# Windowed attention and a SiLU MLP on one core: the first MLP product of the last four token groups made of 7 products of quarters for 8

## The chip, the cores and the metric

One core of a Trainium2 chip runs the whole program. The metric is the device time of one execution in microseconds (us), lower is better, as the median of several runs. TensorE (PE) multiplies, VectorE (DVE) and ScalarE (ACT) work on whole tiles, GpSimd (POOL) takes some elementwise work, and SyncE (SP) issues the transfers.

## What is computed

```python
# attention, 8 batches x 8 heads, 576 positions, head size 64, float32
scores = scale * q @ k^T + bias           # only where 0 <= row - col < 128
attn   = softmax(scores)
x      = (attn @ v) as [4608 tokens, 512]
# MLP
h   = x @ w_in                            # [4608, 512] @ [512, 2048]
g   = h * sigmoid(h)
out = g @ w_out                           # [4608, 2048] @ [2048, 512]
```

## The kernel before

The tokens are cut into 36 tiles of 128 and these into nine groups of 512 tokens (`g` = 0 to 8). For every group the MLP goes through 16 blocks `f` of 128 hidden units. `gemm1` makes the block's hidden values `h` (128 hidden units by 512 tokens) in PSUM, `act1` to `act4` make of them the activated values, and `gemm2` multiplies these with the block's part of `w_out` into four PSUM tiles (`ops`, tags w, x, y, z) that gather over all 16 blocks; `store` scales and writes them. A float32 operand is split into two parts, high and low, and each product is made of three: high by high, high by low, low by high. From group 3 on all of these parts are float16 (`w16`, and `gh`, `gl` for the activated values). So `gemm1` takes, for a block, 4 slices of 128 model dimensions times 3 products, 12 matmuls of 512 columns each; group 2 moves the same columns in pieces of 256 (two matmuls with the same weights, each with a weight load of its own). `gemm2` takes 12 matmuls of 512 columns too. A group has 384 such matmuls.

Attention of group `g + 1` runs inside the MLP of group `g`, one pair (a tile of 128 tokens and four of its heads) for every two blocks. The order of all engines' work is written out by hand: the position `pos` counts half products (64 positions a group), `at(p)` is the position at which pair `p` is begun, and `put` and `later` file each further step under a position. `begin()` issues what is filed for a position, ahead of that position's matmuls. Each engine works through its instructions in the order in which they were issued.

A pair's steps are `scores` (TensorE, into two PSUM tiles of tag a), `row_max` (VectorE), `exps` (ScalarE), `p_hi` and `p_lo` (a float16 split), two transposes by DMA (`p_transpose`), `attend` (TensorE, into one more tile of tag a; this tag has two buffers), `normalize` (VectorE, two stages: the row's divisor, then the division, which frees the tile of tag a), and `x_hi` and `x_lo`, the float16 split of the result. `x_dma` then transposes a finished tile of x, one transfer for each tile from group 1 on, so that it stands ready (tile `xt`) when its group begins. `v_hi` (GpSimd) and `v_lo` (VectorE) split the attention's values, ahead of `attend`. PSUM tag h has two buffers; one block's `h` fills one.

The chain between the products of a block is ScalarE's tanh (L487), VectorE's multiply (L492), ScalarE's float16 copy (L502) and VectorE's remainder (L508). `gemm2` of block `f` is issued behind `gemm1` of block `f + 1`.

Of the kernel before, what the change touches and what calls it, by code (L numbers as in the profile page):

```python
# [16 lines left out]
P = 128  # L17
# [12 lines left out]
TG = 512  # L30
# [33 lines left out]
def at(p):  # L64

    if p < 2 * GT:
        return STEP * (p - 2 * GT) - 18
    if p < 4 * GT:
        return CLOSE[p - 2 * GT]
    return STEP * (p - 2 * GT) - LEAD  # L70


@with_exitstack
def tile_window_attention_then_silu_mlp(ctx, tc, qk, v, w_in, w_out, base8, out):
# [92 lines left out]
    def vscale_finish(b, stage):  # L167

        r, name = vred[b], "".join(str(c) for c in b) if isinstance(b, tuple) else b
        if stage == 0:  # L170
            r["col"] = col = pool.tile([P, 3], F32, tag="vcol", name=f"vcol{name}")
            nc.vector.tensor_reduce(col[:, 0:1], r["m"], axis=AX.X, op=ALU.max)
        elif stage == 1:
            col = r["col"]
            ps = ps_of(next_tag("misc"), f"vt{name}")
            nc.tensor.transpose(ps[:1, :P], col[:, 0:1], ident)
            c = col[:1, 1:2]
            nc.vector.tensor_reduce(c, ps[:1, :P], axis=AX.X, op=ALU.max)
# [9 lines left out]
            nc.vector.tensor_single_scalar(inv.bitcast(I32), c.bitcast(I32), -(14 << 23), op=ALU.add)  # L188
            nc.vector.tensor_scalar(c.bitcast(I32), c.bitcast(I32), -1, 268 << 23, op0=ALU.mult, op1=ALU.add)
# [446 lines left out]
    def put(point, fn, *a):  # L636
        plan.setdefault(max(point, at(0)), []).append((fn, a))

    for p in range(NPAIR):
        i, q = divmod(p, 2)  # L640
        n = at(p)
        if p == 2 * GT - 1:
            a = n + 2 * STEP - 1
        elif p == 2 * GT:
            a = n + 10
        elif p == 2 * GT + 1:
            a = n + 12
        else:
# [32 lines left out]
        put(z + 2, x_lo, p)  # L681
        if q == 0:
# [31 lines left out]
    def later(n, fn, *a):  # L714
        put(pos[0] + n, fn, *a)
# [137 lines left out]
```

## Time and profile before

| | before |
|---|---|
| median of 3 runs | 987.19 us (985.68 to 987.44) |
| the profiled execution, its own time | 983.54 us |
| its span, from the first to the last instruction | 981.8 us |
| mean granted TensorE clock | 0.985 of full speed |

The profile comes from one execution, which was 3.65 us shorter than the median of the three timed runs; 1.7 us of its own time lie around the span. Rows give start and duration in us, or a mean in ns. Matmuls are pipelined and their ends are modelled, so the time that a run of matmuls takes is read from the start of one row to the start of the next.

### The profile page before, as it was taken

Reading aid. Unit: us, or ns where it says so; the run is one execution under the profiler, and the core shown is the slowest. Engines: PE = TensorE matmul, PEld = TensorE weight load, DVE = VectorE, ACT = ScalarE, POOL = GpSimd, SP = SyncE. Lnnn points to the kernel's source line nnn. Section 1 sums busy time; section 2 is a strip of 40 time slices with the busy share of each in tenths; the row PEclk is TensorE's granted clock in tenths of the full one; section 3 lists DMA queues with packets and bytes.
Section 4 is the critical chain, followed back from the end, with each engine's and each line's share of the span. In section 5 each row is a group of like instructions: output and inputs, shape, how many; then the busy total and the mean of one; then the engine's idle time right before and its main releaser. Section 6 shows DMA issues by size and latency. Waiting matters only on the chain.

```text
span 981.8 us, 17277 instructions
## 1 busy us (share of the span) xinstructions
PE 943.0 (96%) x6572; PEld 581.3 (59%) x6572; DVE 625.8 (64%) x1599; ACT 481.9 (49%) x984; POOL 100.2 (10%) x97
## 2 busy tenths in 40 slices
PE   7878889899998999999999999999999999999998
PEld 6756667677776887654555554555555545554443
DVE  4888999755666887776666665554655565553222
ACT  4656666677444554555454444444544454433222
POOL 3112123122111222100000000000000000000000
PEclk8998999999999999999999999999999999999999
DMA  7258886723324542432364545332433343331001
GB/s 233 80 167 222 225 209 186 183 65 86 71 70 129 119 119 76 119 86 65 87 151 118 119 97 129 87 86 65 130 86 87 86 129 87 65 54 54 1 1 43
DMA packets 201074, 104.94 MB, mean 107 GB/s; under 512 B 168224, under 2 KB 176416, under 8 KB 200992
## 3 DMA queue, kind: packets, MB, share of 16 engines
q1 hardware_dynamic: 200992, 103.84, 41.5%
q8 instruction: 52, 0.85, 0.4%
q14 instruction: 30, 0.25, 0.1%
HBM read 54.00 MB, written 9.44 MB: 65 GB/s over the span
## 4 chain that ended last, share of the span: by engine, by line
PE 78%; DVE 12%; DMA 4%; ACT 3%; issue 2%; SPq 1%; POOL 0%; ACTq 0%; DVEq 0%; POOLq 0%
PE o L540 32%; PE h L474 30%; PE sp L278 6%; PE h L479 4%; PE av L368 4%; DVE wm L581 2%; DVE t L298 1%; DVE wm L576 1%; DMA wr<-w_in 1%; DVE gt L492 1%; DMA wr<-w_out 1%; DVE hr L322 1%; DVE wol L595 1%; DVE v L260 1%; DMA hl<-hr 1%
## 5 line engine op out<-in xcount | busy, mean ns | idle before, releaser
L474 PE MATMUL h<-xt,wi 128*128 128x512 f16 (+1 forms) x1536 | 317.8, 354 | 0.0
L487 ACT ACTIVATE gt<-h,gsc 128x512 f32<-128x512 f32 x112 | 77.0, 688 | 318.5 <-PE h L474 316.4
L540 PE MATMUL o<-wo,gh 128*128 128x512 f16 x768 | 228.4, 379 | 0.0
L474 PEld LDWEIGHTS <-wi 128*128 128x128 f16 x1536 | 143.6, 98 | 130.8 <-issue 2.2
L492 DVE SCALAR_TENSOR_TENSOR gt<-gt,h 128x512 f32<-128x512 f32 x144 | 98.6, 685 | 174.4 <-ACT gt L487 174.1
L540 PE MATMUL o<-wo,gl 128*128 128x512 f16 x384 | 145.6, 379 | 0.0
L540 PEld LDWEIGHTS <-gh 128*128 128x128 f16 x768 | 74.8, 98 | 88.6
L308 ACT ACTIVATE t<-t,mx 128x256 f32<-128x256 f32 (+1 forms) x288 | 121.3, 486 | 8.5 <-DVE mx L298 8.5
L508 DVE SCALAR_TENSOR_TENSOR gl<-gt,gh 128x512 f16<-128x512 f32 x96 | 66.4, 692 | 74.8 <-ACT gh L502 74.7
L298 DVE CUSTOM_DVE_ANT_0 t<-sp,tab 128x256 f32<-128x256 f32 (+1 forms) x288 | 102.2, 402 | 18.3 <-PE sp L278 18.0
L322 DVE SCALAR_TENSOR_TENSOR hr<-t,hr 128x512 f16<-128x512 f32 (+1 forms) x128 | 93.5, 748 | 21.4 <-ACT hr L317 21.4
L510 POOL TENSOR_TENSOR gl<-gt,gh 128x512 fp32r<-128x512 f32 x45 | 62.1, 1379 | 287.4 <-ACT gh L500 230.9
L278 PEld LDWEIGHTS sp<-k,q 64*128 64x128 f32 x1088 | 68.8, 190 | 31.9 <-issue 30.2
L278 PE MATMUL sp<-k,q 64*128 64x128 f32 x1088 | 83.2, 289 | 4.6 <-DVE xs L395 4.1
L502 ACT ACTIVATE gh<-gt 128x512 f16<-128x512 f32 x96 | 60.0, 625 | 47.5 <-DVE gt L492 47.2
L540 PE MATMUL o<-woh,gh 128*128 128x512 f32 x192 | 79.2, 413 | 0.7 <-DVE mx L298 0.4
L368 PE MATMUL av<-v,hl 128*128 128x65 f16 (+1 forms) x1632 | 63.9, 195 | 16.1 <-DVE mx L298 10.7
L368 PEld LDWEIGHTS <-hl 128*128 128x128 f16 x1632 | 59.5, 99 | 32.6 <-issue 20.6
L540 PE MATMUL o<-woh,gl 128*128 128x512 f32 x192 | 76.8, 400 | 1.6 <-POOL gl L510 1.6
L317 ACT ACTIVATE hr<-t 128x512 f16<-128x512 f32 (+1 forms) x128 | 75.8, 598 | 1.1 <-DMA hl<-hr 1.1
L540 PE MATMUL o<-wol,gh 128*128 128x512 f32 x192 | 76.3, 398 | 0.0
L249 POOL TENSOR_SCALAR v<-rv,vsc 128x512 f16<-128x512 f32 x32 | 27.6, 861 | 443.7 <-DMA rv<-v 262.0
(108 smaller groups left out, 977.1 us busy)
## 6 DMA issues: line engine op xcount, KB each, us to landing
q<-qk SPq DMA_DIRECT2D x36, 256.0 KB, 3.0
k<-qk SPq DMA_DIRECT2D x36, 256.0 KB, 3.1
vm<-v SPq DMA_DIRECT2D x36, 256.0 KB, 3.6
out<-ot SPq DMA_DIRECT2D x36, 256.0 KB, 2.3
wr<-w_in SPq DMA_DIRECT2D x16, 512.0 KB, 4.0
wr<-w_out SPq DMA_DIRECT2D x16, 512.0 KB, 3.9
rv<-v SPq DMA_DIRECT2D x32, 256.0 KB, 2.9
hl<-hr SPq DMA_TRANSPOSE x128, 2.8
```

The lines of the kernel that those rows point to most:

```text
L278: nc.tensor.matmul(sp[h][:, u, o], qs[i][rows, 2 * q + u], ks[i - 1 + o][rows, 2 * q + u], start=True, stop=True, skip_group_check=True,)
L298: nc.vector.tensor_tensor_reduce(out=t[:, h, 2 * P - n :], in0=st[p]["sp"][h][:, u, o].rearrange("p o c -> p (o c)"), in1=tab[:, 4 * q + 2 ...
L308: nc.scalar.activation(x, x, AF.Exp, bias=st[p]["mx"][:, 2 * u + h : 2 * u + h + 1], scale=-1.0)
L317: nc.scalar.activation(split_of(p, u, hr)[:, 0], t[:, :, 2 * P - n :], AF.Copy, scale=PSCALE)
L322: nc.vector.scalar_tensor_tensor(out=hr[:, 1], in0=t[:, :, 2 * P - n :], scalar=PSCALE, in1=hr[:, 0], op0=ALU.mult, op1=ALU.subtract)
L368: nc.tensor.matmul(av[:, 2 * u + h, : rhs.shape[-1]], lhs, rhs, start=(n == 0), stop=(n == len(seq) - 1), skip_group_check=True,)
L474: nc.tensor.matmul(o, w[:, wp, cc], x, start=start and k == 0, stop=stop, skip_group_check=True)
L487: nc.scalar.activation(gt, hps[n], AF.Tanh, scale=scale)
L492: nc.vector.scalar_tensor_tensor(out=gt, in0=gt, scalar=1.0, in1=hps[n], op0=ALU.add, op1=ALU.mult)
L508: nc.vector.scalar_tensor_tensor(out=gl, in0=gt, scalar=CUT, in1=gh, op0=ALU.mult, op1=ALU.subtract)
L510: (nc.vector if n % NF == NF - 1 else nc.gpsimd).tensor_sub(gl, gt, f32(gh))
L540: nc.tensor.matmul(ops[ti], a[:, t], w, start=(f == 0 and i == 0), stop=(f == NF - 1 and i == len(seq) - 1), skip_group_check=True,)
```

## The change

For groups 5 to 8 the first product is made by Strassen's scheme in Winograd's form. `w_in` is cut into quarters of 256 model dimensions by 1024 hidden units, the group's x into quarters of 256 tokens by 256 model dimensions. Instead of 8 products of quarters there are 7 (P1 to P7), of sums and differences of quarters.

- **TensorE.** A step `j` (0 to 7) makes blocks `j` and `j + 8` of the hidden units together: 7 products of 2 slices times 3 split products, that is 42 matmuls of 256 columns, where two blocks took 24 of 512. `gemm2_7` has the 24 matmuls of 512 columns that two blocks had, one step later than `gemm1_7`, and this order runs on across group borders. A step has 8 positions: one, one, rest, rest, one, rest, one, rest, where "one" are the parts of `gemm1_7` (12, 12, 12 and 6 matmuls) and "rest" those of `gemm2_7` (6 each).
- **VectorE and ScalarE, in every step.** ScalarE copies the bank with P6 and P5 to SBUF (`u`, 512 columns); VectorE adds the bank with P1 and P7 to it (512 columns), and makes three of four halves of the hidden values with three additions of 256 columns; ScalarE copies the fourth (256 columns). The activation chain is as before, from SBUF.
- **The sums of x.** GpSimd makes four sums of 128x256 for every two tiles (`x_sums`), ScalarE and VectorE split them into float16 (two operations of 512 columns each). Two tiles take five transposes by DMA where they took two; those with the sums are issued last.
- **The sums of w_in**, once: in groups 3 and 4, for 8 blocks, 8 GpSimd operations of 128x256 each, 2 ScalarE copies and 2 VectorE subtractions of 512 columns (`w_sum`).
- **Attention's places.** Pairs of groups 5 and up begin 4 positions earlier. With the new order of a step, `attend` (position 3) is issued behind "rest" 0 and `scores` (position 6) behind "rest" 2, both behind matmuls of 512 columns. `attend` of the last two pairs ahead of them moves forward too.
- Two scale constants change by powers of two.

```diff
-    return STEP * (p - 2 * GT) - LEAD
+    return STEP * (p - 2 * GT) - LEAD - (4 if p >= 2 * GT * SEVEN else 0)
...
+    def x_sums(i):
+        a = quarters[i // 2]
+        nc.gpsimd.tensor_add(a[:, 3], a[:, 2], a[:, 3])
+        nc.gpsimd.tensor_sub(a[:, 2], a[:, 0], a[:, 2])
+        nc.gpsimd.tensor_sub(a[:, 0], a[:, 3], a[:, 0])
+        nc.gpsimd.tensor_sub(a[:, 1], a[:, 1], a[:, 0])
...
+    def x_dma7(i, kind):
...
+        nc.sync.dma_start_transpose(pieces[g, "x"][:, c, 2:4].rearrange("p a b c -> p (a b) c"), src[0])
+        for k, n in enumerate(("S3", "S1")):
+            nc.sync.dma_start_transpose(pieces[g][n][:, c], src[1][:, 2 * Q4 * k : 2 * Q4 * (k + 1)])
...
+    def product7(out, g, j, name, start=False):
+        piece, w = {
+            "P1": ("A11", (0, 0)), "P2": ("A12", (0, 2)), "P3": ("S4", (NP7, 2)), "P4": ("A22", (1, 0)),
+            "P5": ("S1", (0, 0, 0)), "P6": ("S2", (1, 1, 0)), "P7": ("S3", (0, 1, 0)),
+        }[name]
+        x = pieces[g][piece]
+        for cc in range(2):
...
+            for k, (wp, xp) in enumerate(((0, 0), (0, 1), (1, 0))):
+                nc.tensor.matmul(
+                    out.rearrange("p (t c) -> p t c", t=2), ws[wp], x[:, :, 2 * xp + cc],
+                    start=start and cc == k == 0, stop=cc == 1 and k == 2, skip_group_check=True,
+                )
+
+    def gemm1_7(g, j, k):
...
+        if k == 0:
+            banks[g, j] = a = [psum.tile([P, TG], F32, tag="h", bufs=2, name=f"h7_{g}_{j}_{n}") for n in range(2)]
+            product7(a[1][:, lo], g, j, "P6", True)
+            product7(a[1][:, hi], g, j, "P5")
...
+            nc.scalar.copy(u, a[1])
+            return
+        a, u = banks[g, j], u7[g, j]
+        if k == 1:
+            product7(a[0][:, lo], g, j, "P1", True)
+            product7(a[0][:, hi], g, j, "P7")
...
+            nc.vector.tensor_add(u, u, a[0])
+            nc.vector.tensor_add(h[1][:, hi], u[:, lo], u[:, hi])
+            return
+        h = h7[g, j]
+        if k == 2:
+            product7(a[0][:, lo], g, j, "P2")
+            product7(a[1][:, hi], g, j, "P3")
+            nc.vector.tensor_add(h[1][:, lo], u[:, lo], a[1][:, hi])
+            for n, x in enumerate((0, 1, 2)):
+                later(n + 1, act7, g, j, x, 1)
+            later(3, act7, g, j, 3, 1)
+            return
+        product7(a[0][:, hi], g, j, "P4")
+        nc.vector.tensor_add(h[0][:, hi], u[:, lo], a[0][:, hi])
+        nc.scalar.copy(h[0][:, lo], a[0][:, lo])
+        for n, x, part in ((1, 0, 0), (1, 1, 0), (2, 2, 0), (2, 3, 0)):
+            later(n, act7, g, j, x, part)
...
+        if i // GT >= SEVEN and q and i % 2:
+            put(z + 3, x_sums, i)
+            for k in range(2):
+                put(z + 5, x_sums_hi, i, k)
+                put(z + 6, x_sums_lo, i, k)
...
+    for f in range(NP7):
+        for k, n in enumerate((0, 3, 6, 11, 12)):
+            put(SUMS + 15 * f + n, w_sum, f, k)
...
+                    one = [(gemm1_7, g, j, k) for k in range(4)]
+                    if before[0] < SEVEN:
+                        seq += [e for k in range(4) for e in (one[k], None)]
+                    else:
+
+                        seq += one[:2] + rest7[:2] + [one[2], rest7[2], one[3], rest7[3]]
```

## Rows read from the trace of the kernel before

**Rows 1.** The page's head, its busy times by engine and the granted clock in 40 slices of 24.5 us.

```profile
span 981.8 us, 17277 instructions
...
PE 943.0 (96%) x6572; PEld 581.3 (59%) x6572; DVE 625.8 (64%) x1599; ACT 481.9 (49%) x984; POOL 100.2 (10%) x97
...
PEclk8998999999999999999999999999999999999999
```

**Rows 2.** The chain of work that ended last, shares of the span by engine and then by line.

```profile
PE 78%; DVE 12%; DMA 4%; ACT 3%; issue 2%; SPq 1%; POOL 0%; ACTq 0%; DVEq 0%; POOLq 0%
PE o L540 32%; PE h L474 30%; PE sp L278 6%; PE h L479 4%; PE av L368 4%; DVE wm L581 2%; DVE t L298 1%; DVE wm L576 1%; DMA wr<-w_in 1%; DVE gt L492 1%; DMA wr<-w_out 1%; DVE hr L322 1%; DVE wol L595 1%; DVE v L260 1%; DMA hl<-hr 1%
```

**Rows 3.** Busy time of each engine by stretch of the span: one stretch in group 4 (501 to 601 us), 5 (603 to 700), 6 (700 to 800) and 8 (894 to 978); columns: stretch, its length, busy us and instructions of PE, PEld, DVE, ACT, POOL, then granted clock, share of the DMA engines, GB/s.

```profile
501.00:601.00 100.00, 99.81 (x714) 51.00 (x713) 63.66 (x184) 45.74 (x93) 3.48 (x4) 1.00 0.53 119
603.00:700.00 97.00, 96.81 (x665) 48.84 (x664) 53.09 (x151) 43.02 (x90) 2.78 (x4) 1.00 0.37 93
700.00:800.00 100.00, 99.81 (x712) 50.99 (x710) 58.12 (x164) 46.05 (x92) 2.78 (x4) 1.00 0.40 96
...
894.00:978.00 84.00, 83.93 (x388) 37.62 (x386) 23.97 (x36) 23.11 (x35) 0.00 (x0) 1.00 0.04 15
```

**Rows 4.** Timeline of TensorE inside group 6, two blocks of 128 hidden units with one attention pair; columns: start us, us, engine, line, operation, tiles, shapes and count. The start of the next row tells how long the products of a row were streamed; the second column contains the modelled end.

```profile
716.82 2.76 PE L474 MATMUL h<-xt,wi 128*128 128x512 f16 x12
719.42 0.59 PE L540 MATMUL o<-wo,gh 128*128 128x512 f16 x2
...
722.01 1.46 PE L474 MATMUL h<-xt,wi 128*128 128x512 f16 x6
723.30 0.89 PE L368 MATMUL av<-v,hl 128*128 128x65 f16 x24
724.03 1.46 PE L474 MATMUL h<-xt,wi 128*128 128x512 f16 x6
725.32 0.59 PE L540 MATMUL o<-wo,gh 128*128 128x512 f16 x2
...
728.00 1.16 PE L278 MATMUL sp<-k,q 64*128 64x128 f32 x16
729.10 2.76 PE L474 MATMUL h<-xt,wi 128*128 128x512 f16 x12
```

**Rows 5.** Timeline of TensorE inside group 2, where the first MLP product moves 256 columns, and the weight loads (PEld) of the same stretches; columns as in rows 4.

```profile
311.03 1.49 PE L474 MATMUL h<-xt,wi 128*128 128x256 f16 x12
312.35 0.89 PE L368 MATMUL av<-v,hl 128*128 128x65 f16 x24
...
318.35 2.79 PE L474 MATMUL h<-xt,wi 128*128 128x256 f16 x24
320.90 0.48 PE L540 MATMUL o<-woh,gh 128*128 128x512 f32 x1
...
312.24 0.87 PEld L368 LDWEIGHTS <-hl 128*128 128x128 f16 x24
...
318.35 2.52 PEld L474 LDWEIGHTS <-wi 128*128 128x128 f16 x24
```

**Rows 6.** Instructions by line and form in groups 5 to 7 (603 to 894 us): line, engine, operation, tiles, shapes, count, then busy us and mean ns of one, then idle time before; the last line is that of L422 over the whole span (duration ns min/median/max).

```profile
L502 ACT ACTIVATE gh<-gt 128x512 f16<-128x512 f32 x48 | 30.0, 624 | 22.1 <-DVE gt L492 22.1
...
L411 DVE TENSOR_TENSOR x<-xs,x 128x256 f16<-128x256 f32 x24 | 10.1, 419 | 5.1 <-ACT x L405 5.1
L395 DVE TENSOR_TENSOR xs<-av,r 128x256 f32<-128x256 f32 x24 | 10.0, 418 | 0.1
...
L422 DVE TENSOR_TENSOR xl<-xp,xh x4: 678/686/692, 47.2 to 55.9; 128x512 fp32r<-128x512 f32 x4
```

**Rows 7.** Timeline of group 8, the chain from the first product to the second of one block of hidden units; columns as in rows 4, and in brackets the idle time before and what ended it.

```profile
967.31 0.59 PE L540 MATMUL o<-wo,gh 128*128 128x512 f16 x2
...
967.57 0.69 ACT L487 ACTIVATE gt<-h,gsc 128x512 f32<-128x512 f32 x1 [3.11 <-PE h L474]
...
968.29 0.69 DVE L492 SCALAR_TENSOR_TENSOR gt<-gt,h 128x512 f32<-128x512 f32 x1 [3.10 <-ACT gt L487]
...
969.01 0.63 ACT L502 ACTIVATE gh<-gt 128x512 f16<-128x512 f32 x1 [0.76 <-DVE gt L492]
...
969.67 0.69 DVE L508 SCALAR_TENSOR_TENSOR gl<-gt,gh 128x512 f16<-128x512 f32 x1 [0.69 <-ACT gh L502]
```

**Rows 8.** GpSimd's subtraction on the page, and VectorE's subtraction of line 411 between 60 and 170 us, when GpSimd is busy; columns as in rows 6.

```profile
L510 POOL TENSOR_TENSOR gl<-gt,gh 128x512 fp32r<-128x512 f32 x45 | 62.1, 1379 | 287.4 <-ACT gh L500 230.9
...
L411 DVE TENSOR_TENSOR x<-xs,x 128x256 f16<-128x256 f32 x7 | 5.2, 738 | 0.0
```

**Rows 9.** SyncE's issue of the transposes of x (L434) and of attention's weights (L330; a few of them have half the size), as duration ns min/median/max, and the median us from issue to landing of those of x.

```profile
L434 SPq DMA_TRANSPOSE xt<-x x32: 1231/1233/2374, 177.3 to 887.7; - x32
...
L330 SPq DMA_TRANSPOSE hl<-hr x128: 1189/1233/2370, 65.7 to 873.7; - x128
...
xt<-x SPq DMA_TRANSPOSE x32, 2.8
```

**Rows 10.** TensorE's idle time ahead of group 2 (timeline) and the stretch behind it (busy time by stretch, columns as in rows 3).

```profile
302.87 1.13 PE L278 MATMUL sp<-k,q 64*128 64x128 f32 x14 [3.47 <-DVE xs L395]
...
304.00:310.00 6.00, 6.00 (x32) 4.54 (x33) 5.31 (x15) 2.19 (x5) 1.30 (x1) 0.72 0.18 52
```

More of the change, by code (lines that the diff above doesn't have):

```diff
@@ L408, in x_lo @@
         i, q = divmod(p, 2)
-        if i >= XD:
+        if i // GT >= SEVEN:
+            if (i % 2, q) != (1, 0):
+                piece = xt[i][:, q * (1 - i % 2)]
+                nc.vector.tensor_sub(piece[:, 1], st[p]["x"], piece[:, 0])
+                if q == 1:
+                    whole.append((i, "own"))
+        elif i >= XD:
             cols = slice(q * 4 * D, (q + 1) * 4 * D)
@@ L414, in x_lo, with x_sums_hi @@
         del st[p]
+    quarters = {}
+    def x_sums(i):
[4 more added lines that the diff above has]
+        nc.gpsimd.tensor_sub(a[:, 1], a[:, 1], a[:, 0])
+    def x_sums_hi(i, k):
+        xt[i, "sums", k] = t = pool.tile([P, 2, 2, Q4], F16, tag="x", bufs=4, name=f"xsum{i}_{k}")
+        nc.scalar.copy(t[:, :, 0], quarters[i // 2][:, 2 * k : 2 * k + 2])
@@ new lines, in x_sums_lo @@
+    def x_sums_lo(i, k):
+        t = xt[i, "sums", k]
+        nc.vector.tensor_sub(t[:, :, 1], quarters[i // 2][:, 2 * k : 2 * k + 2], t[:, :, 0])
+        if k == 1:
+            whole.append((i, "sums"))
+    def x_dma7(i, kind):
+        g, c = i // GT, i % GT // 2
+        if (g, "x") not in pieces:
+            pieces[g, "x"] = four = pool.tile(
+                [P, 2, 4, 4, P], F16, tag="xh" if g % 2 else "xl", bufs=1, name=f"xq4_{g}"
+            )
+            pieces[g] = {n: four[:, :, k] for k, n in enumerate(("A11", "A12", "S2", "S4"))}
+            for k, n in enumerate(("A22", "S3", "S1")):
+                pieces[g][n] = pool.tile(
+                    [P, 2, 4, P], F16, tag=f"{'wol' if g % 2 else 'woh'}{NP7 + k}", bufs=1, name=f"{n}_{g}"
+                )
+        if kind == "own":
+            src = xt[i].rearrange("p a b c -> p (a b c)")
+            if i % 2:
+                nc.sync.dma_start_transpose(pieces[g]["A22"][:, c], src[:, : 2 * Q4])
+            else:
+                nc.sync.dma_start_transpose(pieces[g, "x"][:, c, 0:2].rearrange("p a b c -> p (a b) c"), src)
+            return
+        src = [xt[i, "sums", k].rearrange("p a b c -> p (a b c)") for k in range(2)]
+        nc.sync.dma_start_transpose(pieces[g, "x"][:, c, 2:4].rearrange("p a b c -> p (a b) c"), src[0])
+        for k, n in enumerate(("S3", "S1")):
+            nc.sync.dma_start_transpose(pieces[g][n][:, c], src[1][:, 2 * Q4 * k : 2 * Q4 * (k + 1)])
@@ new lines, in tile_window_attention_then_silu_mlp, with w_sum @@
+    sums, pieces = {}, {}
+    def w_sum(f, stage):
+        spare = f + 1 if f < NP7 - 1 else NF - 1
+        if stage == 0:
+            sums[f] = b = [
+                pool.tile([P, 2, Q4], F32, tag=f"{kind}{spare}", bufs=1, name=f"wq{f}_{kind}") for kind in ("woh", "wol")
+            ]
+        else:
+            b = sums[f]
+        if stage < 2:
+            for k in range(2):
+                w = w16[0, f + NP7 * stage].rearrange("p a b c -> p a (b c)")
+                nc.gpsimd.tensor_add(
+                    b[k][:, stage], w[:, 0, Q4 * k : Q4 * (k + 1)], w[:, 1, Q4 * k : Q4 * (k + 1)]
+                )
+        elif stage == 2:
+            nc.gpsimd.tensor_sub(b[0][:, 0], b[0][:, 1], b[0][:, 0])
+            nc.gpsimd.tensor_sub(b[0][:, 1], b[1][:, 1], b[0][:, 1])
+            nc.gpsimd.tensor_sub(b[1][:, 1], b[1][:, 1], b[0][:, 0])
+            nc.gpsimd.tensor_sub(b[1][:, 0], b[1][:, 0], b[1][:, 1])
+        elif stage == 3:
+            w7[f] = [
+                pool.tile([P, 2, 2, Q4], F16, tag=f"{kind}{f}", bufs=1, name=f"w7{f}_{kind}") for kind in ("woh", "wol")
+            ]
+            for k in range(2):
+                nc.scalar.copy(w7[f][k][:, :, 0], b[k])
+        else:
+            for k in range(2):
+                nc.vector.tensor_sub(w7[f][k][:, :, 1], b[k], w7[f][k][:, :, 0])
@@ new lines, in act7 @@
+    def act7(g, j, stage, part):
+        h = h7[g, j][part]
+        if stage == 0:
+            gact[g, j, part] = gt = pool.tile([P, TG], F32, tag="gt", name=f"gt{g}_{j}_{part}")
+            nc.scalar.activation(gt, h, AF.Tanh, scale=gsc[g][:, 0:1])
+            return
+        gt = gact[g, j, part]
+        if stage == 1:
+            nc.vector.scalar_tensor_tensor(out=gt, in0=gt, scalar=1.0, in1=h, op0=ALU.add, op1=ALU.mult)
+            return
+        if (g, j) not in gact:
+            gact[g, j] = [pool.tile([P, 2, TG], F16, tag=f"g{c}", name=f"g{c}{g}_{j}") for c in "hl"]
+        gh, gl = (t[:, part] for t in gact[g, j])
+        if stage == 2:
+            nc.scalar.activation(gh, gt, AF.Copy, scale=CUT)
+        else:
+            nc.vector.scalar_tensor_tensor(out=gl, in0=gt, scalar=CUT, in1=gh, op0=ALU.mult, op1=ALU.subtract)
@@ new lines, in gemm2_7 @@
+    def gemm2_7(g, j, k):
+        half, part = k // 2, 1 - k % 2
+        for ti in (2 * half, 2 * half + 1):
+            if j == 0 and part:
+                ops[ti] = psum.tile([P, DM], F32, tag="wxyz"[ti], name=f"o{g}_{ti}")
+            gh, gl = (t[:, part] for t in gact[g, j])
+            w = w16[1, j + NP7 * part]
+            t = slice(ti % 2 * Q4 + ti // 2 * P, ti % 2 * Q4 + ti // 2 * P + P)
+            for i, (a, wp) in enumerate(((gh, 0), (gh, 1), (gl, 0))):
+                nc.tensor.matmul(
+                    ops[ti], a[:, t], w[:, wp], start=j == 0 and part == 1 and i == 0,
+                    stop=j == NP7 - 1 and part == 0 and i == 2, skip_group_check=True,
+                )
+        if j == NP7 - 1 and part == 0:
+            store(g, 2 * half)
+            store(g, 2 * half + 1)
@@ L439, in x_send @@
             return
-        for i in [i for i in whole if i // GT <= now[0] + 1]:
-            whole.remove(i)
-            x_dma(i)
+        for a in [a for a in whole if (a[0] if isinstance(a, tuple) else a) // GT <= now[0] + 1]:
+            whole.remove(a)
+            if isinstance(a, tuple):
+                x_dma7(*a)
+            else:
+                x_dma(a)
     def x_parts(i, part):
```

52 lines of the change are left out of this document (49 added, 3 removed).

## The prediction, made before the changed kernel was run

> **What bounds the kernel.** I read the page's busy times first. TensorE is busy for 943.0 of 981.8 us, but matmul ends are modelled, so that alone proves little [rows 1]. The chain that ended last is the better witness: 78% of it is TensorE, 12% VectorE, and the two longest lines are the two MLP products [rows 2]. The change acts in groups 5 to 8, so I then took stretches there: TensorE is busy for 96.8 of 97 us, 99.8 of 100 and 83.9 of 84 at a granted clock of 1.00, while VectorE has 53 to 58 us of work and GpSimd 3 [rows 3]. In the timeline the matmuls follow each other without a gap [rows 4]. So in these groups the time is the sum of what TensorE streams; everything else fits beneath it. A shorter stream shortens the kernel unless another engine is late.
>
> **The products.** A pair of blocks streams 12 + 6 + 6 matmuls of 512 columns in 2.60 + 1.29 + 1.29 us (716.82 to 719.42, 722.01 to 723.30, 724.03 to 725.32), 5.18 us or 215.8 ns each [rows 4]. The change removes 8 steps x 24 x 4 groups = 768 of them, 165.7 us, and adds 8 x 42 x 4 = 1344 of 256 columns. Group 2 already runs that form, a weight load ahead of each: 24 take 2.55 us, 106.3 ns each, and 12 ahead of an attend take 1.32 us, 110 ns [rows 5]. 106.3 ns is 256 columns at 2.4 GHz, so the load hides completely. That loads can go still faster is seen beside it: 24 of attend's take 0.87 us [rows 5]. I take 106.3 ns, from the longer run: 142.9 us. With 110 ns it would be 147.8. The products give 165.7 - 142.9 = **22.8 us** (17.9 at the other end). The second product keeps its matmuls, only in another order.
>
> A rule of the Trainium skill stands against the lower price: TensorE: Matmul & The Clock Gate, section Back-to-back issue gap, gives 262 cycles for 256 columns and 518 for 512. At 2.4 GHz that is an estimate of 109.2 ns, and the sum would be 165.7 - 146.7 = 19.0 us. The row of 24 shows 106.3, so I keep the row.
>
> **What a step must do now.** Before, two blocks with a full pair take 729.10 - 716.82 = 12.28 us [rows 4]. A step after takes 12.28 - 5.18 + 42 x 0.1063 = 11.56 us. In it, from its start: one 0 to 1.3, one to 2.6, rest to 3.8, attend (0.73) to 4.6, rest to 5.9, one to 7.1, rest to 8.4, scores (1.10 and a short gap) to 9.6, one to 10.2, rest to 11.5.
>
> VectorE's new work: the 512-column addition from PSUM 0.69 (as L422), three of 256 columns at 0.42 (as L395), and 2 x 0.69 in every fourth step for the sums of x [rows 6]: 2.3 us a step. Before it had 58.1 / 8 = 7.3 [rows 3], so 9.6 of 11.56 us, 83%. ScalarE: 46.1 / 8 = 5.8 [rows 3], plus copies of 0.62 and 0.39, and 0.31 for the sums [0.62 from rows 6; 0.39, which is not in a row, I set at 0.62 as its upper end]: at most 7.4. Neither is the bound by its sum; the cover is 2 us on VectorE. What is left are single waits:
>
> - P2 writes a bank that VectorE must have read for `u`. One1 ends at 2.6; a result is seen by the next engine 0.26 us after the next matmul starts (967.31 to 967.57 [rows 7]); the addition ends at 3.5, P2 starts at 5.9. Hidden.
> - The last part's chain: 10.2 + 0.26 + 0.42, then tanh to remainder, 967.57 to 969.67 and 0.69 more, 2.8 us [rows 7]: 13.7. The second product asks for it at 11.56 + 4.6 = 16.2. Hidden, with 2.4 us for queueing.
> - `scores` needs the bank that the division of `normalize` frees. On VectorE this division stands behind the addition that follows the third "one": 7.1 + 0.26 + 0.42 + 0.42 = 8.2 against scores at 8.4. That is the thinnest cover. When the sums of x (1.4 us) run in the same step VectorE may arrive late. I take 0.2 us for the 6 steps of groups 5 to 7 that have them, 1.2 us. Ends: nothing, and 0.3 us in all 24 steps with attention, 7.2.
> - A group's start. P6 and P5 come first and read S2 and S1, which are transposed last. On VectorE their split stands behind `v_lo` and two additions, so it ends near 6.0 us in step 7. SyncE then issues one transpose of attention and S2, S3, S1, 1.23 us each, and half the size costs no less there (minimum 1189 ns); a transpose lands 2.8 us after its issue [rows 9]. S1 is issued at about 9.9 and lands at 12.7; P5 wants it at 11.56 + 0.64 = 12.2. 0.5 us at the starts of groups 6 and 7; group 8's has no attention in its way, and group 5's follows the old, longer order. 1.0 us in all; ends 0 and 4.
> - The start of group 5 has no second product between the second and third "one". P2 there waits about 3.5 - 3.3; with old work in VectorE's queue I take 0.5 us (ends 0.2 and 1.5).
> - GpSimd's sums of w_in: 64 operations, by half of the 1379 ns of 512 columns 0.69 us each [rows 8], 44 us in groups 3 and 4 (88 us if the half costs as much as the whole). While GpSimd works, VectorE's subtraction of two SBUF tiles takes 738 ns [rows 8] and not 419 [rows 6]. VectorE has 36 us to spare in 100 there [rows 3], so most is hidden: 0.5 us; ends 0 and 4. The sums of x take 4 x 0.69 = 2.8 us, begun at 9.3 in a step and asked for 4 us later: nothing; at 1.38 each they would hold `v_hi`, `v_lo` and so `attend` by some 0.8 us, six times.
> - The end of group 8: the last half waits for its chain, 0.2 us more than before.
>
> Moving attention by 4 positions keeps it behind 512-column products, where scores stand already; its matmuls cost the same, so nothing. The constants cost nothing: the same instructions run.
>
> **Sum.** 22.8 - 1.2 - 1.0 - 0.5 - 0.5 - 0.2 = **19.4 us** gained. The profiled execution's 983.5 would become 964.1; the median of the runs shown is 3.65 higher, so I predict 987.2 - 19.4 = **967.8**.
>
> **Rivals.**
> - *TensorE waits in every step with attention* (the scores case at its far end): 0.3 us x 24 rather than 1.2, so 967.8 + 6.0 = 973.8. For it: 0.2 us of cover and VectorE at 83%. Against: the divisor and the split of attention's weights are done well before the third "one" ends. 0.18.
> - *256 columns cost 110 ns.* 967.8 + 4.9 = 972.7. For it the shorter run of group 2, against it the longer. 0.09.
> - *The transposes land late at every group's start.* 10 a group for 4. SyncE issues in order, so one late wait ahead of S2 delays all three; 5 us at each of four starts gives back 20 us: no change, 987. Against: even my worst order above is late by 0.5. 0.03.
> - *VectorE becomes the bound, slower.* If it can't fill its waits inside the two chains of a step (tanh 0.72 and copy 0.69 twice, 2.8 us) and waits four times 0.26 us for TensorE, a step takes 9.6 + 2.8 + 1.0 = 13.4 us, and 24 steps give (13.4 - 11.56) x 24 = 44 us: 1012. It decides from 19.4 / 24 = 0.8 us a step, a VectorE round of 12.4 us. Against: in group 6 those gaps already hold attention's work, with 42 us idle in 100. 0.04.
> - *Loads are not hidden.* 576 loads more, at group 2's pace of 2.52 / 24 us of loading time, 0.105 each [rows 5], cost 60 us: 967.8 + 60 = 1028. Group 2's dense 256-column run speaks against it. 0.01.
>
> The last is what the Trainium skill would have, TensorE: Matmul & The Clock Gate, section on packing small matmuls: a load overlaps a running matmul only in another row group of the array. Here all use the whole array; by that rule group 2 could not show 106.3 ns for a load and a matmul together, so this trace disagrees.
>
> A fall of the granted clock needs a long wait first: 0.72 after TensorE had sat idle for 3.47 us [rows 10]. No wait above is as long, so I give that nothing of its own.
>
> **How the numbers follow.** My forecast has 0.65; the rivals 0.18, 0.09, 0.03, 0.04 and 0.01. About 0.2%, 2 us, is what a measurement of this kernel can tell from no change. Faster: 0.65 + 0.18 + 0.09 = 0.92; same 0.03; slower 0.05. The range starts where the products give 22.8 and only the start of group 5 costs (0.2), with 1 us for the runs' scatter: 963.5. It ends past the first rival, 975.5. The likeliest case alone is 964 to 971.
>
> **What would show it.** 1344 matmuls of 128x256 at about 106 ns from start to start; a step with attention of 11.6 us and one of group 8 of 9.6; groups 5 to 8 shorter by about 5 us each, groups 0 to 4 unchanged. Idle time on TensorE ahead of scores by VectorE's division, or ahead of P5 by a transpose, would show the two waits. I'm wrong if a step comes out at 12.3 us or if 256 columns take more than 110 ns.

## The result, and the profile after

The changed kernel took 991.92 us (989.88 to 994.42, six runs) beside 985.82 (984.56 to 987.44, six runs) of the kernel before: ratio 1.006, 95% interval 1.0043 to 1.0076. I had forecast 967.8; it is 6.1 us slower. The profiled execution took 992.12 us, against the 964.1 that the forecast gave for it, so 28 us have to be found.

The page of after, its head, busy times, granted clock by slice, and the chain's shares by engine:

```profile
span 990.3 us, 18847 instructions
...
PE 932.3 (94%) x7148; PEld 641.1 (65%) x7148; DVE 711.8 (72%) x1751; ACT 521.3 (53%) x1072; POOL 183.2 (18%) x193
...
PEclk8989999999999999999999899999999999999999
...
PE 69%; DVE 16%; ACT 5%; DMA 5%; issue 3%; SPq 1%; POOL 0%; ACTq 0%; DVEq 0%; POOLq 0%
```

TensorE is busy for 10.7 us less than in [rows 1], yet the span is 8.5 us longer: TensorE waits. The chain names for whom: VectorE has 16% of it, 12% in [rows 2]. The page does not say where. For that I took one mark, the start of group 5's first product, in before and then in after:

```profile
603.67 2.75 PE L474 MATMUL h<-xt,wi 128*128 128x512 f16 x12
```

```profile
624.49 0.82 PE L529 MATMUL h<-xq,w_wol 128*128 128x256 f16 x6
```

Ahead of it after is 20.8 us longer, behind it 12.3 us shorter (378.1 to 365.8). 2.0 of the 20.8 us lie ahead of group 3, in code that the change does not touch. So **groups 3 and 4, which I had priced at 0.5 us, lost 18.8**, 1.2 of them the scores of one pair that the new places move there, out of group 5.

Busy time by stretch of after (columns as in [rows 3]), then the same of before for its groups 3 and 4:

```profile
403.00:514.00 111.00, 106.61 (x720) 55.32 (x719) 85.51 (x208) 59.07 (x120) 32.91 (x42) 0.98 0.36 92
514.00:624.00 110.00, 104.06 (x706) 53.02 (x705) 73.31 (x190) 50.28 (x100) 26.07 (x34) 0.95 0.47 111
563.00:573.00 10.00, 9.69 (x42) 4.98 (x43) 4.16 (x15) 3.89 (x9) 3.72 (x6) 0.71 0.44 110
624.00:990.00 366.00, 356.33 (x2964) 241.03 (x2961) 247.77 (x608) 180.07 (x362) 33.38 (x35) 1.00 0.33 81
```

```profile
403.00:603.00 200.00, 198.51 (x1401) 101.46 (x1400) 134.44 (x369) 97.59 (x197) 6.26 (x8) 1.00 0.44 105
```

TensorE's idle time in groups 3 and 4 is 4.4 + 5.9 = 10.3 us, 1.5 before: 8.8 more. The granted clock is 0.98 and 0.95 where it was 1.00; by an estimate from these rows that is 0.02 x 111 + 0.05 x 110 = 7.7 us of streaming (0.5 us a row either way by rounding). Together 16.5 of the 17.6 us that are left without the moved scores. VectorE is idle for 25 and 37 us in these two stretches, so it is no bound by its sum. TensorE's waits there (403 to 624 us), as us, times, longest:

```profile
PE sp L283 <- DVE xq L404: 6.6, 3, 3.4
PE sp L283 <- DVE xs L404: 2.5, 3, 1.6
...
```

Nearly all is one kind of wait: `scores` (L283) for the division of `normalize` (L404), which frees its bank of tag a. I had seen this wait, but for groups 5 to 7.

The longest of them on TensorE:

```profile
559.44 0.48 PE L283 MATMUL sp<-k,q 64*128 64x128 f32 x2
563.31 2.04 PE L283 MATMUL sp<-k,q 64*128 64x128 f32 x14 [3.38 <-DVE xq L404]
565.29 4.51 PE L666 MATMUL h<-xt,wi 128*128 128x512 f16 x12
569.63 0.59 PE L732 MATMUL o<-wo,gh 128*128 128x512 f16 x2
```

`scores` writes into its first bank and then waits 3.38 us for the second. Behind the wait, twelve matmuls of 512 columns take 569.63 - 565.29 = 4.34 us instead of 2.60 [rows 4]: the granted clock of 563 to 573 us is 0.71 (table above). VectorE in the same time:

```profile
555.50 1.20 DVE L700 SCALAR_TENSOR_TENSOR gl<-gt,gh 128x512 f16<-128x512 f32 x1 [2.00 <-ACT gh L694]
556.62 2.34 DVE L455 TENSOR_TENSOR xsum<-xq,xsum 128x512 f16<-128x512 f32 x2
558.89 1.28 DVE L327 SCALAR_TENSOR_TENSOR hr<-t,hr 128x512 f16<-128x512 f32 x2
560.09 0.68 DVE L513 TENSOR_TENSOR w_woh<-wq_woh,w_woh 128x512 f16<-128x512 f32 x1
...
561.30 0.15 DVE L391 TENSOR_SCALAR r<-av 128x4 f32<-128x4 f32 x1
...
562.74 0.42 DVE L404 TENSOR_TENSOR xq<-av,r 128x256 f32<-128x256 f32 x1
```

`attend`, whose result the division takes, was done when TensorE went on at 555.46; the division still stands behind the remainder (L700), the split of the sums of x (L455), that of attention's weights (L327) and that of the sums of w_in (L513). The idle 2.00 us ahead of L700 is no spare time: the queue is in order, and nothing behind the waiting instruction can use it.

### The profile page after: what moved, and what is told of

It reads as the page before. It is cut to its first block, busy times and chain, and to the rows that moved or that the text cites. A ratio compares the mean times of both kernels' runs of the same rounds, so it can differ in the third digit from the quotient of the medians.

```text
span 990.3 us, 18847 instructions
## 1 busy us (share of the span) xinstructions
PE 932.3 (94%) x7148; PEld 641.1 (65%) x7148; DVE 711.8 (72%) x1751; ACT 521.3 (53%) x1072; POOL 183.2 (18%) x193
## 4 chain that ended last, share of the span: by engine, by line
PE 69%; DVE 16%; ACT 5%; DMA 5%; issue 3%; SPq 1%; POOL 0%; ACTq 0%; DVEq 0%; POOLq 0%
PE o L732 14%; PE o L597 14%; PE h L529 13%; PE h L666 12%; PE sp L283 7%; PE h L671 5%; PE av L373 4%; DVE wm L773 2%; DVE hr L327 2%; DVE t L303 2%; ACT t L313 1%; DVE wm L768 1%; DMA wr<-w_in 1%; DMA vm<-v 1%; DVE gt L684 1%
## 5 line engine op out<-in xcount | busy, mean ns | idle before, releaser
L666 PE MATMUL h<-xt,wi 128*128 128x256 f16 (+1 forms) x768 | 141.1, 334 | 0.0
L327 DVE SCALAR_TENSOR_TENSOR hr<-t,hr 128x512 f16<-128x512 f32 (+1 forms) x128 | 97.5, 779 | 24.8 <-ACT hr L322 24.4
L303 DVE CUSTOM_DVE_ANT_0 t<-sp,tab 128x256 f32<-128x256 f32 (+1 forms) x288 | 103.1, 402 | 10.3 <-DMA tab<-base 6.3
L666 PEld LDWEIGHTS <-wi 128*128 128x128 f16 x768 | 72.6, 100 | 49.8 <-issue 6.6
L283 PE MATMUL sp<-k,q 64*128 64x128 f32 x1088 | 89.1, 292 | 15.9 <-DVE xs L404 8.3
L283 PEld LDWEIGHTS sp<-k,q 64*128 64x128 f32 x1088 | 72.9, 192 | 44.6 <-issue 43.0
L574 ACT ACTIVATE gt<-hs,gsc 128x512 f32<-128x512 f32 x64 | 45.9, 716 | 102.8 <-DVE hs L559 102.8
L679 ACT ACTIVATE gt<-h,gsc 128x512 f32<-128x512 f32 x48 | 33.0, 687 | 124.9 <-PE h L666 122.8
L597 PE MATMUL o<-wo,gl 128*128 128x512 f16 x256 | 97.0, 379 | 0.1
L684 DVE SCALAR_TENSOR_TENSOR gt<-gt,h 128x512 f32<-128x512 f32 x80 | 54.6, 683 | 48.9 <-ACT gt L679 48.4
L529 PE MATMUL h<-xq,wi 128*128 128x256 f16 x576 | 73.3, 273 | 1.3 <-DVE u L552 1.3
L597 PEld LDWEIGHTS <-gh 128*128 128x128 f16 x512 | 48.5, 98 | 35.7 <-ACT gh L584 0.6
```

Of the source, the lines that this page charges most:

```text
L283: nc.tensor.matmul(sp[h][:, u, o], qs[i][rows, 2 * q + u], ks[i - 1 + o][rows, 2 * q + u], start=True, stop=True, skip_group_check=True,)
L303: nc.vector.tensor_tensor_reduce(out=t[:, h, 2 * P - n :], in0=st[p]["sp"][h][:, u, o].rearrange("p o c -> p (o c)"), in1=tab[:, 4 * q + 2 ...
L327: nc.vector.scalar_tensor_tensor(out=hr[:, 1], in0=t[:, :, 2 * P - n :], scalar=PSCALE, in1=hr[:, 0], op0=ALU.mult, op1=ALU.subtract)
L529: nc.tensor.matmul(out.rearrange("p (t c) -> p t c", t=2), ws[wp], x[:, :, 2 * xp + cc], start=start and cc == k == 0, stop=cc == 1 and k ...
L597: nc.tensor.matmul(ops[ti], a[:, t], w[:, wp], start=j == 0 and part == 1 and i == 0, stop=j == NP7 - 1 and part == 0 and i == 2, skip_gro ...
L666: nc.tensor.matmul(o, w[:, wp, cc], x, start=start and k == 0, stop=stop, skip_group_check=True)
```

## The experiments

Where each kernel's time lies, from its profiled execution, in us; a group ends here with the start of the next group's first product on TensorE, the mark used above. Scatter of the first column (406 to 411) is that of equal code. Group 3 of the kernels with the new places has the scores of one pair (1.2 us) that before, e2, e3 and e8 have later. The first product of e3's group 5 waits 3.86 us for a transpose, which stands in its column of group 4.

| kernel | to end of group 2 | group 3 | group 4 | groups 5 to 8 | span |
|---|---|---|---|---|---|
| before | 406.4 | 97.4 | 99.9 | 378.1 | 981.8 |
| after | 408.4 | 105.6 | 110.5 | 365.8 | 990.3 |
| e1 no sums of w_in | 408.7 | 100.7 | 101.9 | 366.2 | 977.4 |
| e2 before + sums of w_in | 409.3 | 100.3 | 100.1 | 378.1 | 987.9 |
| e3 places back | 410.0 | 100.5 | 108.9 | 395.1 | 1014.5 |
| e4 no sums of x | 409.7 | 104.2 | 100.5 | 361.7 | 976.0 |
| e9 GpSimd's half | 410.5 | 102.7 | 105.5 | 364.8 | 983.6 |
| e10 the split half | 410.5 | 102.5 | 107.8 | 366.3 | 987.1 |
| e6 sums spread | 409.2 | 103.3 | 109.7 | 365.9 | 988.1 |
| e5 division first | 409.0 | 101.0 | 104.2 | 370.6 | 984.8 |
| e7 both | 409.9 | 101.9 | 103.5 | 370.7 | 986.0 |
| e8 before, division first | 408.4 | 97.6 | 99.8 | 378.1 | 983.9 |
| e11 division first, b | 408.7 | 101.3 | 104.0 | 363.7 | 977.7 |
| e12 sums gated | 407.2 | 102.0 | 100.6 | 368.4 | 978.1 |

### Which part costs it: one part out, or one part alone

**e1**, no sums of w_in:

```diff
-    for f in range(NP7):
-        for k, n in enumerate((0, 3, 6, 11, 12)):
-            put(SUMS + 15 * f + n, w_sum, f, k)
```

> The changed kernel without the sums of w_in (products P4 to P7 take unsummed parts of w_in; that part of the computation is left out, matmuls and all else stay). Theory W (the sums of w_in put ScalarE copies and VectorE subtractions ahead of normalize's division in groups 3 and 4, scores wait for it): most of the 17.6 us lost there come back, 974 to 980 us. Theory P (attention's earlier places make the waits): 988 to 992. Theory X (the sums of x make them): 984 to 990.

980.37 us, ratio 0.994 (0.9921 to 0.996): the sums of w_in cost 11.5 us of the changed kernel. The same chain on VectorE, and the wait that it ends, in e1:

```profile
550.83 0.69 DVE L702 SCALAR_TENSOR_TENSOR gl<-gt,gh 128x512 f16<-128x512 f32 x1 [2.32 <-ACT gh L696]
551.44 1.29 DVE L455 TENSOR_TENSOR xsum<-xq,xsum 128x512 f16<-128x512 f32 x2
552.65 1.29 DVE L327 SCALAR_TENSOR_TENSOR hr<-t,hr 128x512 f16<-128x512 f32 x2
...
555.30 0.42 DVE L404 TENSOR_TENSOR xq<-av,r 128x256 f32<-128x256 f32 x1
```

```profile
555.87 1.13 PE L283 MATMUL sp<-k,q 64*128 64x128 f32 x14 [0.61 <-DVE xq L404]
```

From the remainder to the division: 4.47 us here, 562.74 - 555.50 = 7.24 in after, 2.77 more. Start to start, the remainder takes 0.51 us longer, the two operations of L455 1.06, and the two of L513 add 1.21: 2.78. The wait grew from 0.61 to 3.38, by 2.77. So this wait is accounted for: 1.21 us is new work of VectorE, 1.57 us other work that takes longer; that GpSimd is what makes it longer, e9 shows below.

**e2**, the sums of w_in alone, added to the kernel before, their results unused:

```diff
+    for f in range(NP7):
+        for k, n in enumerate((0, 3, 6, 11, 12)):
+            put(SUMS + 15 * f + n, w_sum, f, k)
```

> The kernel before with the sums of w_in added and used by nothing. Theory W: 6 to 15 us slower than before, TensorE waiting ahead of scores in groups 3 and 4. Theories P and X: within 2 us of before.

990.05 us, ratio 1.004 (1.0027 to 1.0053). That is 3.5 us above the runs of before beside it. Between the marks nearly all of it lies in group 3 (100.3 us for 97.4); group 4 took 100.1, before 99.9.

**e4**, no sums of x: the transposes read plain tiles instead.

```diff
-            put(z + 3, x_sums, i)
-            for k in range(2):
-                put(z + 5, x_sums_hi, i, k)
-                put(z + 6, x_sums_lo, i, k)
+            put(z + 6, lambda i: whole.append((i, "sums")), i)
```

> The changed kernel without the sums of x (GpSimd's four sums and their split left out; the same number of transposes reads the tile's own parts instead). Theory X: 975 to 980 us. Theory W: 980 to 989, the two long waits of group 4 shorter since one of two causes of the queue is gone, those of group 3 as they were. Theory P: 989 to 993.

979.33 us, ratio 0.9927 (0.9908 to 0.9946). Over before's groups 3 and 4 with the moved scores (197.3 + 1.2 = 198.5), after is 17.6 us longer, e1 4.1 and e4 6.2. One by one the two sums cost 10.3, together 17.6: they do not add. The cover that each of them uses up, seen in an ordinary step of e1, on VectorE and then on TensorE:

```profile
541.33 0.42 DVE L404 TENSOR_TENSOR xq<-av,r 128x256 f32<-128x256 f32 x1
...
542.49 1.16 PE L283 MATMUL sp<-k,q 64*128 64x128 f32 x16
```

The division ends at 541.75 and scores asks for its bank at 542.49, 0.74 us. What fits into that costs nothing; what comes on top is a wait. TensorE's idle time in groups 3 and 4, from mark to mark, is 3.7 us in e1, 4.4 in e4 and 9.3 in after. The granted clock stayed at 1.00 in both groups of e1 and of e4, so the loss by the clock came only with both sums together.

**e3**, attention's places as before:

```diff
-    return STEP * (p - 2 * GT) - LEAD - (4 if p >= 2 * GT * SEVEN else 0)
+    return STEP * (p - 2 * GT) - LEAD
...
-        elif 2 * GT * SEVEN - 2 <= p < 2 * GT * SEVEN:
-            a = n + (9 if q else 10)
```

> The changed kernel with attention's places as before (no 4 positions earlier, attend 13 positions behind scores throughout). Theory P: the waits of groups 3 and 4 go, 975 to 980 us. Theory W or X: 986 to 994, at most the wait of 2 us at the place where the shift begins is saved.

1014.97 us, ratio 1.0277 (1.0247 to 1.0307). The move, which I had priced at nothing, saves 23 us. TensorE's waits in e3 from 610 us on:

```profile
PE h L529 <- DMA xq<-xsum: 12.2, 4, 3.9
...
PE h L529 <- DMA S<-xsum: 4.2, 4, 1.4
```

Without it the last x of a group is finished too late: its sums and five transposes have to be done when the next group's first product begins, and at each of the four starts TensorE waits for them; the granted clock is 0.97 from 610 us to the end, where after has 1.00.

### Which half of the sums of w_in

**e9** makes GpSimd's 64 sums but neither copies nor splits them; **e10** copies and splits tiles that hold no sums. e9 then multiplies with the plain w_in, as e1; e10 with the split of those other tiles.

```diff
-        for k, n in enumerate((0, 3, 6, 11, 12)):
+        for k, n in enumerate((0, 3, 6)):
```

```diff
-            b = sums[f]
+            b = [f32(weight(kind, spare)).rearrange("p (a c) -> p a c", a=2) for kind in ("woh", "wol")]
...
-        for k, n in enumerate((0, 3, 6, 11, 12)):
+        for k, n in ((3, 11), (4, 12)):
```

> The changed kernel with GpSimd's 64 operations of the sums of w_in kept and their split on ScalarE and VectorE left out (products P4 to P7 take unsummed parts of w_in, so that part of the computation is left out). Without any of it the time was 980.4 us. Theory L (GpSimd runs its operations as soon as their inputs are there, in a burst, and VectorE's operations with two SBUF operands take about twice their time beside them, 1.2 us for 0.6): 985 to 991, most of the 11.5 us. Theory Q (the split's place in the queues): at most 982.

> The changed kernel with the split of the sums of w_in on ScalarE and VectorE kept, reading w_out's float32 parts instead, and GpSimd's sums left out. Theory Q: 986 to 992. Theory L: 980 to 984. If both halves give less than 4 us over 980.4, only the two together make the loss.

e9: 985.79 us, ratio 0.9995 (0.9983 to 1.0007). e10: 988.62, 1.0031 (1.0017 to 1.0045). Over e1 that is 5.4 and 8.2 us, 11.5 with both. Neither half is innocent: GpSimd alone, with no instruction of these sums on VectorE, costs 5 us. In groups 3 and 4 the halves lie 5.7 and 7.7 us above e1, after 13.5. The longest wait comes apart in the same way; TensorE in e9, then in e10:

```profile
561.33 1.13 PE L283 MATMUL sp<-k,q 64*128 64x128 f32 x14 [2.17 <-DVE xq L404]
```

```profile
560.72 1.64 PE L283 MATMUL sp<-k,q 64*128 64x128 f32 x14 [1.81 <-DVE xq L404]
```

That is 1.56 and 1.20 us more than the 0.61 of e1: the 1.57 and 1.21 worked out above. VectorE in e9, where it has no work of these sums:

```profile
554.74 1.20 DVE L702 SCALAR_TENSOR_TENSOR gl<-gt,gh 128x512 f16<-128x512 f32 x1 [2.00 <-ACT gh L696]
555.86 2.34 DVE L455 TENSOR_TENSOR xsum<-xq,xsum 128x512 f16<-128x512 f32 x2
```

In e10, without GpSimd's work, the same two rows have 0.69 and 1.29.

The longest wait of group 3 has another maker, ScalarE. In after:

```profile
480.13 0.60 ACT L510 CAST w_woh<-wq_woh 128x512 f16<-128x512 f32 x1
...
481.16 0.62 ACT L694 ACTIVATE gh<-gt 128x512 f16<-128x512 f32 x1
481.81 0.69 DVE L700 SCALAR_TENSOR_TENSOR gl<-gt,gh 128x512 f16<-128x512 f32 x1 [2.63 <-ACT gh L694]
482.43 0.42 DVE L404 TENSOR_TENSOR xs<-av,r 128x256 f32<-128x256 f32 x1
482.99 1.56 PE L283 MATMUL sp<-k,q 64*128 64x128 f32 x14 [1.64 <-DVE xs L404]
```

ScalarE's two copies for the sums stand ahead of `gh` and put it off by 1.03 us; VectorE waits for `gh` with the division behind it in the queue. `scores` waits 1.64 us here, 0.68 in e1, 0.60 in e9 (no copies) and 1.71 in e10 (copies).

### Other places for the sums

**e6** spreads GpSimd's three stages over a whole step and puts the copies and splits where I saw room:

```diff
-        for k, n in enumerate((0, 3, 6, 11, 12)):
-            put(SUMS + 15 * f + n, w_sum, f, k)
+        c = 210 + 16 * f + (4 if f > 1 else 0)
+        for k, n in enumerate((-17, -15, -9, 0, 3)):
+            put(c + n, w_sum, f, k)
```

> The changed kernel with the sums of w_in at other positions: ScalarE's copies where it idles (behind scores), VectorE's subtractions ahead of the remainder (L700) for which it waits anyway, GpSimd's four differences away from the positions ahead of the division. The same instructions. Theory Q: 980 to 984 us, as without these sums. Rival C: 988 to 992, as GpSimd does as much.

990.3 us, ratio 1.0049 (1.0032 to 1.0067): as slow as after. VectorE and GpSimd in e6:

```profile
552.62 1.22 DVE L513 TENSOR_TENSOR w_woh<-wq_woh,w_woh 128x512 f16<-128x512 f32 x1
...
554.90 1.21 DVE L700 SCALAR_TENSOR_TENSOR gl<-gt,gh 128x512 f16<-128x512 f32 x1
```

```profile
551.42 0.73 POOL L501 TENSOR_TENSOR wq_woh<-wq_woh 128x256 f32<-128x256 f32 x1
552.23 1.06 POOL L502 TENSOR_TENSOR wq_woh<-wq_wol,wq_woh 128x256 f32<-128x256 f32 x1
553.37 1.06 POOL L503 TENSOR_TENSOR wq_wol<-wq_wol,wq_woh 128x256 f32<-128x256 f32 x1
```

GpSimd's operations still run one behind the other, from 546.38 to 559 us without a pause: a position only orders its queue, and here GpSimd had nothing to wait for and ran ahead. While both work, each operation is held: VectorE's with two SBUF operands take 1.21 us instead of 0.69 [rows 7], GpSimd's 1.06 instead of 0.73.

### The division earlier

**e5** puts the division one position earlier from group 3 on, and the sums of x with it; **e7** is e5 with e6's places; **e8** is the kernel before with the division's part of e5.

```diff
-        put(z + 1, normalize, p, 1)
-        put(z + 2, x_hi, p)
-        put(z + 2, x_lo, p)
+        late = p < 2 * GT * 3
+        put(z + late, normalize, p, 1)
+        put(z + 1 + late, x_hi, p)
+        put(z + 1 + late, x_lo, p)
...
-            put(z + 3, x_sums, i)
+            put(z + 2, x_sums, i)
...
-                put(z + 5, x_sums_hi, i, k)
-                put(z + 6, x_sums_lo, i, k)
+                put(z + 4, x_sums_hi, i, k)
+                put(z + 5, x_sums_lo, i, k)
```

> The changed kernel with both stages of normalize issued together from group 3's pairs on, ahead of the activation chain's multiply, and the split of x and its sums one position earlier. Theory Q (VectorE works in order; what stands ahead of the division makes scores wait, and the sums of x and of w_in only add to that queue): 974 to 982 us, the long waits of group 4 under 1.5 us each, the waits for S at the starts of groups 6 and 7 gone. Rival C (the sums cost because VectorE and GpSimd hold each other up, whatever the order): 988 to 992.

> Both edits together. Theory Q: 970 to 976 us: 985.8 less 19.0 for the products at 109.2 ns, plus about 3 for group 5's start and 2 for what is left. Rival C: 986 to 990.

> The kernel before with the division moved in the same way. Theory Q: within 1.5 us of before, since nothing waits for the division there. If it gains more than 3 us, the gain of the division's place is no part of the change's story.

e5: 986.2 us, ratio 0.9998 (0.9984 to 1.0011); e7: 987.29, 1.0014 (1.0003 to 1.0024), the spread sums gaining nothing here either; e8: 985.66, 0.9992 (0.9978 to 1.0006). The place of the division is worth nothing to the kernel before, so e5 does remove a loss of the change: its groups 3 and 4 are 10.9 us shorter than after's. But groups 5 to 8 became 4.8 us longer. A row of e5 on TensorE:

```profile
652.84 0.76 PE L373 MATMUL av<-v,hl 128*128 128x64 f16 x20 [1.67 <-DVE v L265]
```

The split of the sums of x, moved forward, now stands ahead of `v_lo`, and `attend` waits for that: 9.2 us in six waits behind the start of group 5, 0.8 in one in after. **e11** is e5 with that split left where it was, and with `attend` of two pairs one position earlier:

```diff
+        elif p in (2 * GT * SEVEN, 2 * GT * (SEVEN + 1)):
+            a = n + 12
```

> As e5_division_first, but the split of the sums of x back at its old positions (ahead of it GpSimd's sums one earlier), and attend of two pairs one position earlier, ahead of the old group's last activation chain. In e5 attend waited four times 1.67 us for v_lo behind the earlier split; without that and the waits at the ends of groups 3 and 4: 976 to 981 us. If the division's place and v_lo are not the cause, 985 or more.

**979.86 us, ratio 0.9935 (0.9919 to 0.9952)**: 12.1 us below after and faster than the kernel before. Where after had its longest wait, e11 has the division straight behind its divisor:

```profile
556.54 0.15 DVE L391 TENSOR_SCALAR r<-av 128x4 f32<-128x4 f32 x1
...
556.93 0.42 DVE L404 TENSOR_TENSOR xq<-av,r 128x256 f32<-128x256 f32 x1
```

0.39 us from divisor to division, 1.44 in after. Its groups 3 and 4 are still 6.8 us above the 198.5, with waits of TensorE of 4.4 us in all, for VectorE, ScalarE and a transpose, none over 1.6 us. A third buffer of tag a, so that scores need not wait for the division, was not tried. **e12** is e11 with GpSimd's sums held back: four at a time, behind a one-column operation that reads a pair's finished split, with the copies and splits filed by pairs too.

```diff
+            nc.gpsimd.tensor_scalar(gate, lo, vsc[i // NBLK][:, 0:1], 1.0, op0=ALU.mult, op1=ALU.mult)
+            f, half = divmod(STEPS.index(p), 2)
+            for k in ((2,) if half else (0, 1)):
+                w_sum(f, k)
```

> e11 with the sums of w_in let go by a one-column operation of GpSimd that reads the finished split of a pair, four sums for each pair, so that GpSimd works where VectorE has single-SBUF-operand work, and the split of these sums behind scores. Theory L: 2 to 5 us below e11, 973 to 978. Theory Q alone: as e11.

981.19 us, ratio 0.9948 (0.9933 to 0.9963): no better than e11. The waits for the division are gone, and groups 3 and 4 are 2.7 us shorter than e11's, but groups 5 to 8 are 4.7 longer. Other waits have come; the longest on TensorE in e12:

```profile
477.51 0.89 PE L374 MATMUL av<-v,hl 128*128 128x65 f16 x24 [3.54 <-DVE mx L304]
```

## Why the prediction was wrong

The 28 us, by the prediction's own steps: 17.1 in groups 3 and 4, 8.8 in groups 5 to 8, 2.0 ahead of group 3 in equal code, of the size that the first column of the table scatters by.

**The sums of w_in: the step that failed.** I wrote "VectorE has 36 us to spare in 100 there [rows 3], so most is hidden: 0.5 us; ends 0 and 4". It was 17.6 us, together with the sums of x for group 5, which are made in group 4 too and which I had priced at nothing (e1, e2, e4). Four things were wrong in it. I compared a sum of work with a sum of idle time, where the cover is that of one instruction: the division's, 0.74 us in e1. I did look at the division's cover, but only in the steps of groups 5 to 7, where I took 1.2 us; there no scores waited behind the first step. I had the row that showed VectorE slower beside GpSimd, and let the idle sum take that as well; e9 shows it to cost 5.4 us, with no instruction added on VectorE. ScalarE's copies I did not price at all; they make the longest wait of group 3. And "No wait above is as long, so I give that nothing of its own" left out the clock, by the estimate above 7.7 us, nearly half of the loss: the waits that go before its fall were not in the list. Nor does the length of a wait settle it: in the trace of before the granted clock was 0.57 from 106 to 110 us, behind a wait of 2.03 us, shorter than the 3.47 I went by. GpSimd's operations themselves, which I took at 0.69 us, were 0.73 alone and 1.06 when held.

**The price of 256 columns: mis-sized, 3.8 us.** TensorE of after, a step of group 5:

```profile
646.05 0.82 PE L529 MATMUL h<-xq,w_wol 128*128 128x256 f16 x6
...
648.67 0.59 PE L597 MATMUL o<-wo,gh 128*128 128x512 f16 x2
...
657.74 0.82 PE L529 MATMUL h<-xq,w_wol 128*128 128x256 f16 x6
```

24 matmuls take 2.62 us, 109.2 ns each: 146.7 us for 1344, and the products give 19.0, not 22.8. It is what the Trainium skill gives (TensorE: Matmul & The Clock Gate, Back-to-back issue gap, 262 cycles), which I had set aside for the row of 24 in [rows 5]. That row ends at the start of a float32 matmul; the trace then has 0.32 us to the next float32 start, and 0.23 or 0.24 between the later ones, so I take that start to be recorded some 0.08 us early. A run of 12 ahead of such a start is short by as much (325.84 to 327.07 in before, 1.23 us where 12 x 109.2 ns are 1.31), so the error lies in the end of a run and not in each matmul. The shorter run of [rows 5], ended by a float16 matmul, was right with 110. With 109.2 the step is 12.28 - 5.18 + 4.59 = 11.69 us, and 657.74 - 646.05 is 11.69.

**Waits in groups 5 to 8.** TensorE's, from 624 us on:

```profile
PE h L529 <- DMA S<-xsum: 1.7, 3, 0.8
PE h L529 <- DVE u L552: 1.3, 1, 1.3
PE av L373 <- DVE v L265: 0.8, 1, 0.8
PE h L529 <- DMA xq<-xsum: 0.7, 1, 0.7
PE sp L283 <- DVE xq L404: 0.5, 1, 0.5
```

The transposes at the group starts cost 2.4 us where I took 1.0 (ends 0 and 4). The first two steps of group 5 cost 1.3 + 0.8 + 0.5 = 2.6 where I took 0.5, beyond my end of 1.5: I had the wait for `u`, not the two that come behind it. `scores` waits once, not in six steps. These and the price give 3.8 + 1.4 + 2.1 - 1.2 = 6.1 of the 8.8 us. Eight of the attends from 661 us on add 1.8; they take up to 0.96 us:

```profile
661.65 1.11 PE L373 MATMUL av<-v,hl 128*128 128x65 f16 x24
662.60 0.59 PE L597 MATMUL o<-wo,gh 128*128 128x512 f16 x2
```

where the others take 0.72. What holds these eight no run settled; 0.9 us is open besides.

**What held.** The loads hide: 1344 matmuls, each with a load of its own, at 109.2 ns. Neither VectorE nor ScalarE became the bound of a step, and the chains inside a step fitted. Behind the mark the change gains 12.3 us, 11.1 without the moved scores. Of the signs that I named, the step (11.69 us for 11.6) came near enough; "groups 0 to 4 unchanged" is the one that failed.

**Moving attention** was right at nothing for its matmuls, and wrong as a part: undone it costs 23 us (e3), since the move pays for the late sums of x. I had priced the move and never what stands without it.

## What to carry to other kernels

Work that fits into an engine's idle sum is hidden only if it fits ahead of the next instruction that somebody waits for: find, in the engine's queue, the release with the least cover, in every stage that gets new work, and price against that one number the new work of every engine on the way to it (here VectorE, GpSimd beside it, and ScalarE ahead of it). Put releases first in a queue that is in order, and look at what the instruction that they displace releases in turn (e5 against e11). Elementwise work on GpSimd is not free for VectorE while VectorE's operations read two SBUF tiles (e9: 5.4 us).

## What was new about the hardware

- VectorE and GpSimd hold each other: 0.69 us became 1.21 for VectorE's operations with two SBUF operands, 0.73 became 1.06 for GpSimd's (rows of e6), while VectorE's multiply with one operand in PSUM kept a mean of 683 ns in groups 3 and 4 of e6. The Trainium skill has that rule (SBUF — State Buffer, Who interferes with whom: a VectorE instruction with two SBUF inputs contends with a GpSimd one that reads SBUF; one with at most one SBUF input, outside the two-port modes, does not), and these rows agree. I had the first sign of it, 738 ns against 419 in [rows 6, 8].
- A wait of 3.38 us was followed by a granted clock of 0.71 over 563 to 573 us, and one of 1.64 us (482.99) by twelve matmuls of 512 columns in 3.79 us instead of 2.60: 1.7 and 1.2 us more on top of the waits. The same wait of 1.64 us in e4 (484.42) was followed by a granted clock of 1.00 and twelve matmuls in 2.60 us, so a wait of that length did not always cost this.
- A float32 matmul behind float16 ones seems to be recorded about 0.08 us early (runs of 24 and of 12 matmuls come out short by 0.07 and 0.08 us); a run of matmuls is better read between two starts of one kind.
